# Layer-norm sums by bn_stats, broadcasts by DMA, transposes two products late, and the next slab's gradient of h ahead of each weight gradient, in a fused gated long convolution with its gradients

## The chip, the cores and the metric

The kernel runs on one core of a Trainium2 chip, and the metric is its device time in microseconds (us). One execution computes a forward output and nine gradients. All arrays are bf16 in memory; matrix products accumulate in f32.

## The reference

`x` is 2048 rows by 1024 columns, the three weights connect 1024 and F = 3584 columns. The forward part, cut to what is computed:

```python
xn = (x - mean(x)) / sqrt(var(x) + 1e-5)            # layer norm over the 1024 columns
k_shift = sum over t of k[rows - (3 - t)] * shift_k  # four taps per column
kv  = k_shift * v
y   = irfft(rfft(kv padded to 4096) * rfft(ssm_k padded)) [:2048] + kv * ssm_D
s   = xn * y
h   = (xn @ w_gate) * (xn @ w_up)                    # 2048 x 3584
g   = silu(h @ w_down)
out = x + s * g
```

Then come the gradients of `out`, for a given `grad_out`, by `x`, `k`, `v`, `shift_k`, `ssm_k`, `ssm_D`, `w_gate`, `w_up` and `w_down`. The ten arrays are the outputs.

## The kernel before

Rows are taken in 16 blocks of 128, which make four quarters `q` of 512; the 1024 columns are 8 chunks `dc`; F is 28 chunks `fc` of 128, and two chunks make a slab of 256 columns, of which there are 14. The work follows this order:

- *Start and first two slabs.* `ln_load` fetches the rows of x in chunks of 1, 1, 2, 4, 4 and 4 blocks. `layer_norm` (L408) takes a chunk's row sums on DVE (L412), its sums of squares on ACT (L418), some ten small operations, one of them a square root on ACT (L431), then subtracts and scales each block on DVE (L446, L447), transposes it on PE (L450) and copies the result to `XNT[q]` (L451; the tiles that the trace calls `U`). Once a quarter is there, `gu_unit` multiplies it with the four chunks of the first two slabs. After quarter 0 `build_bcast` (L125) spreads the four taps `shift_k` and the row `ssm_D` to all 128 partitions (`Wbc`, `Dbc`): it copies a tap to a row on one partition (L132), multiplies it with a row of ones on PE (L137), and ACT copies the product from PSUM (L138). After quarter 1 `build_tables` (L145) makes the tables of sines `TF` and, by transposes on PE (L172) and copies on ACT (L173), `TI`.
- *Forward loop.* `gu_unit` (L460) for chunks 4 to 27 and two quarters at a time: four products `psg` of 8 matmuls each (gate and up of each quarter), a copy of each to `gut` on ACT (L472), and on DVE the product `hT` (L478), which goes to memory as `HTd`, and, transposed on PE (L486), as `Hd`. The transposition is a closure `turn` in the list `later`, which `flush` (L456) runs after the next product. After each product `tick` lets `conv_forward`, the convolution by Fourier transforms on PE and DVE, advance by a share of its work: `pump(cnt[0] / NT)` with `NT = 24 * 8.0`, where 192 is the number of products in this loop. What is not done at the end, `drain` does.
- *Middle.* w_down is loaded, `ht` (256 rows of `HTd`) is loaded, and `psbm` = h @ w_down is formed block by block; `gate` makes the output and the gradients that come back through it. `dbm` is transposed into `DBMT` by the same `later` list (L845).
- *Gradient loop*, over the 14 slabs. `dh_half` (L902), four times a slab (two chunks, two halves `hf` of the rows), loads `gul` = the stored gate and up products, forms two products `psdh`, the gradient of h (ACT copies them to `dht`, L913), and on DVE `dgt` = `gul` * `dht` (L917). `dgt` goes to memory, and a `turn` transposes it in two groups of 8 (L925), which ACT copies into `dgu` (L926). `dw_slab` (L929) then forms the gradients of w_up and w_gate: 8 products `psdw` of 16 matmuls, each copied by ACT to `wb` (L937) and stored. `load_wdt` (L891) loads and transposes the slab's rows of w_down. `btick` lets `conv_backward` advance. `dgu` rotates over three tiles.
- *End.* `dwd_slab` forms the gradient of w_down, and the last stage the gradient of xn (`psx`) with the layer norm's backward.

A scheduler puts each engine's instructions into an order of its own choice within what the dependences allow. Loads go by `ld` on SP's queue, most others by `st` and `cld` on POOL's queue; the two first weight slabs are issued by ACT. The loop of the gradients stands as follows:

```python
for sl in range(NSL):
    dgus = []
    for hf in range(2):
        dgu = u8(4 + nd % 3, "p (b a f) -> p b a f", b=8, a=2)
        nd += 1
        for fi in range(2):
            dh_half(2 * sl + fi, hf, wdt, dgu)
        dgus.append(dgu)
    if sl + 1 < NSL:
        wdt = load_wdt(sl + 1)
    flush()
    dw_slab(sl, dgus)
```

Of the kernel before, what the change touches and what calls it, by code (L numbers as in the profile page):

```python
# [19 lines left out]
def build_kernel(  # L20
# [33 lines left out]
    o_dshk, o_dssmk, o_dD, o_dwg, o_dwu, o_dwd = out_4, out_5, out_6, out_7, out_8, out_9  # L54

# [69 lines left out]
    def build_bcast(bps):  # L125
        bsb = pool("bc_sb", 1)
        row = bsb.tile([1, 5, D], BF16, name="row")
        st(row[:, 4, :], A_ssm_D.rearrange("(o d) -> o d", o=1))
        shrow = bsb.tile([1, D, 4], BF16, name="shrow")
        st(shrow[:], A_shift_k.rearrange("(o d) j -> o d j", o=1))  # L130
        for j in range(4):
            nc.vector.tensor_copy(row[0:1, j, :], shrow[0:1, :, j])  # L132
# [7 lines left out]
        nc.vector.memset(zr[:], 0.0)  # L140
# [4 lines left out]
    def build_tables(psp):  # L145
# [20 lines left out]
        for g in range(2):  # L166
            for rp in range(4):
# [5 lines left out]
                nc.scalar.copy(out=TI[:, g, 2 * rp:2 * rp + 2].rearrange("p i k (c u) -> p i k c u", c=2), in_=ps[:])  # L173
        tg.release()


    V = nc.vector
# [230 lines left out]
    def layer_norm(b0, n, x4):  # L408
        def small(name, dt=F32):
            return lns.tile([P, 4], dt, name=name)[:, 0:n]  # L410
        ssum = small("ssum")
        V.tensor_reduce(ssum, x4[:, 0:n, :], AX.X, ADD)  # L412
        negmean = small("negmean")
        V.tensor_scalar(negmean, ssum, -1.0 / D, None, op0=MUL)
        sqs = small("sqs")
        for i in range(n):
            junk = lnp.tile([P, D], BF16, name="junk", bufs=2)
            nc.scalar.activation(junk[:], x4[:, i, :], ACT.Square, bias=negmean[:, i:i + 1], scale=1.0,  # L418
                                 accum_out=sqs[:, i:i + 1])
        mean_b = small("mean_b", BF16)  # L420
        V.tensor_scalar(mean_b, negmean, -1.0, None, op0=MUL)
# [3 lines left out]
        V.tensor_scalar(var_b, sqs, 1.0 / D, None, op0=MUL)  # L425
# [17 lines left out]
        for i in range(n):  # L443
# [7 lines left out]
            V.tensor_copy(XNT[q][:, :, qi * P:(qi + 1) * P], ps[:])  # L451
# [4 lines left out]
    def flush():  # L456
        while later:
            later.pop(0)()
# [135 lines left out]
    for c in xs[:3]:  # L594
        layer_norm(*c)
    for q in range(4):
        if q > 0:
            layer_norm(*xs[q + 2])
# [562 lines left out]
```

## Time and profile before

| | |
|---|---|
| time, median of 3 runs | 2392.72 us (2388.26 to 2396.47) |
| profiled execution: time, span | 2397.11 us, 2395.3 us |
| mean granted TensorE clock of it | 0.979 |
| busy: PE, DVE, ACT, POOL | 92%, 60%, 36%, 25% of the span |
| memory traffic | 450.67 MB, mean 188 GB/s |

PE is TensorE's matmuls (transposes are matmuls too), PEld its weight loads, which run beside them, DVE is VectorE, ACT ScalarE, POOL GpSimd, SP SyncE. A row of a timeline gives start, length, engine, line, operation, out<-in, shapes and count, and in brackets how long the engine stood idle before it and what ended the wait. A row of a waits view gives who waited, for whom, the sum in us, how often, and the longest. A row of a group gives busy us and mean ns behind the bar, then the idle time ahead of the group. A row of stages gives the window, its length, the busy us (and instructions) of PE, PEld, DVE, ACT and POOL, the granted clock, the share of the DMA engines and the GB/s that they moved. The profiler's page cuts the span into 40 slices of 60 us and gives tenths.

### The profile page before, as it was taken

To read this page: it belongs to the slowest core of one execution; us is meant where nothing else is said; L and a number is where in the kernel's file an instruction comes from. 1 tells how busy PE (TensorE), PEld (TensorE's weight loads), DVE (VectorE), ACT (ScalarE), POOL (GpSimd) and SP (SyncE) were. 2 spreads that over 40 slices of the span, in tenths; PEclk is the share of its full clock that TensorE was granted. 3 is DMA by queue.
4 is the path that set the end of the run, shared out by engine and by line. 5 is a ranking of instruction groups with operands and counts; after the bars stand their busy time and mean duration, and the time that the engine had idled before them with its cause. 6 is when DMAs were issued, how large, how long until landed. Compare 5 with 4: busy or idle time off the path is not lost.

```text
span 2395.3 us, 35474 instructions
## 1 busy us (share of the span) xinstructions
PE 2206.5 (92%) x14370; PEld 1185.8 (50%) x14634; DVE 1443.0 (60%) x1941; ACT 863.7 (36%) x1197; POOL 590.7 (25%) x923
## 2 busy tenths in 40 slices
PE   4799999999979997999899989999999999999997
PEld 2456565666634444555455544444454455444443
DVE  8468879796836555666786866777747601322222
ACT  6734443444414234333333334345341152211111
POOL 3532313222202222222344444322224310000000
PEclk9899999999989999999999999999999999999999
DMA  8365747455467657445666566555647665432321
GB/s 271 131 227 177 234 150 257 163 194 180 167 243 258 247 203 280 160 169 138 201 205 217 192 207 223 169 185 195 232 169 239 206 198 187 164 144 101 110 98 35
DMA packets 195285, 450.67 MB, mean 188 GB/s; under 512 B 36224, under 2 KB 93608, under 8 KB 183088
## 3 DMA queue, kind: packets, MB, share of 16 engines
q0 software_dynamic: 71776, 270.11, 32.9%
q1 hardware_dynamic: 119184, 176.18, 22.8%
q8 instruction: 114, 1.87, 0.3%
q10 hardware_dynamic: 4160, 2.10, 0.3%
q14 instruction: 51, 0.42, 0.1%
HBM read 258.48 MB, written 194.02 MB: 189 GB/s over the span
## 4 chain that ended last, share of the span: by engine, by line
PE 41%; issue 25%; DVE 13%; DMA 9%; POOL 6%; ACT 5%; another core or an unknown queue 0%; POOLq 0%; SPq 0%; ACTq 0%; DVEq 0%
PE psx L1049 12%; PE psdw L933 10%; PE psdw L993 5%; PE psg L470 3%; DVE W L185 3%; DMA out_dram<-wb 2%; PE psdh L911 2%; DVE m L185 2%; POOL out_dram L60 2%; PE tr L925 2%; DMA DGUTd<-dgt 1%; PE psbm L808 1%; DVE HX L185 1%; PE tr L981 1%; DMA HFd<-HX 1%
## 5 line engine op out<-in xcount | busy, mean ns | idle before, releaser
L470 PE MATMUL psg<-U,wslab 128*128 128x512 bf16 x1709 | 406.6, 385 | 9.1 <-DVE U L451 3.6
L933 PE MATMUL psdw<-U,U 128*128 128x512 bf16 x1737 | 400.3, 380 | 14.7 <-ACT wb L937 9.3
L1049 PE MATMUL psx<-U,dgut 128*128 128x512 bf16 x1376 | 305.6, 379 | 1.7
L1049 PEld LDWEIGHTS <-dgut 128*128 128x128 bf16 x1792 | 174.7, 98 | 208.1
L933 PEld LDWEIGHTS <-U 128*128 128x128 bf16 x1792 | 172.8, 98 | 199.2 <-issue 9.5
L470 PEld LDWEIGHTS <-wslab 128*128 128x128 bf16 x1792 | 173.0, 99 | 196.5 <-issue 17.8
L60 POOL DMA_DIRECT2D out_dram<-wb x280 | 151.5, 546 | 303.6 <-ACT wb L937 192.0
L472 ACT CAST gut<-psg 128x512 bf16<-128x512 f32 x224 | 131.2, 586 | 250.5 <-PE psg L470 233.0
L185 DVE TENSOR_TENSOR W<-W 128x512 f32<-128x512 f32 (+1 forms) x272 | 213.5, 785 | 7.3
L911 PE MATMUL psdh<-U,wdt 128*128 128x512 bf16 x857 | 210.2, 383 | 5.2 <-ACT dht L913 3.3
L808 PE MATMUL psbm<-U,ht 128*128 128x512 bf16 x875 | 196.9, 382 | 7.7 <-DMA ht<-HTd 6.4
L993 PE MATMUL psdw<-U,U 128*128 128x512 bf16 x873 | 199.3, 380 | 3.5 <-ACT wb L996 1.4
L185 DVE TENSOR_TENSOR W<-W,psP 128x512 f32<-128x512 f32 x192 | 122.6, 683 | 120.7 <-PE psP L234 66.9
L937 ACT CAST wb<-psdw 128x512 bf16<-128x512 f32 x112 | 65.6, 586 | 283.2 <-PE psdw L933 225.1
L185 DVE TENSOR_TENSOR dxn<-psx,dxna_t 128x1024 f32<-128x1024 f32 x16 | 19.6, 1225 | 220.8 <-PE psx L1049 204.3
L926 ACT COPY U<-tr 128x1024 bf16<-128x1024 bf16 x112 | 113.4, 1013 | 84.6 <-PE tr L925 84.4
L808 PEld LDWEIGHTS <-ht 128*128 128x128 bf16 x896 | 87.6, 99 | 110.6 <-DMA ht<-HTd 6.6
L993 PEld LDWEIGHTS <-U 128*128 128x128 bf16 x896 | 86.7, 98 | 100.7 <-issue 2.8
L911 PEld LDWEIGHTS <-wdt 128*128 128x128 bf16 x896 | 84.3, 99 | 84.4 <-issue 5.5
L1065 ACT ACTIVATE junk<-dxn 128x1024 bf16<-128x1024 f32 x16 | 16.9, 1057 | 279.7 <-DVE dxn L185 279.7
L185 DVE TENSOR_TENSOR m<-A,B 128x2048 bf16<-128x2048 bf16 x64 | 75.8, 1221 | 63.6 <-DMA B<-KFd 27.1
L60 POOL DMA_DIRECT2D out_dram<-dx_t x16 | 8.6, 540 | 402.0 <-DVE dx_t L1077 402.0
(250 smaller groups left out, 3105.9 us busy)
## 6 DMA issues: line engine op xcount, KB each, us to landing
gul<-GUTd SPq DMA_DIRECT2D x56, 512.0 KB, 5.4
DGUTd<-dgt POOLq DMA_DIRECT2D x56, 512.0 KB, 6.6
dgut<-DGUTd SPq DMA_DIRECT2D x16, 1792.0 KB, 8.7
GUTd<-gut POOLq DMA_DIRECT2D x48, 512.0 KB, 3.7
A<-DYFd POOLq DMA_DIRECT2D x16, 1024.0 KB, 5.5
ht<-HTd SPq DMA_DIRECT2D x8, 1792.0 KB, 7.4
out_dram<-wb POOLq DMA_DIRECT2D x224, 64.0 KB, 2.1
U<-Hd SPq DMA_DIRECT2D x28, 512.0 KB, 4.2
```

What stands on the lines that cost most here:

```text
L60: return nc.gpsimd.dma_start(out=out, in_=in_)
L185: V.tensor_tensor(o, a, b, op)
L470: nc.tensor.matmul(ps[:], w[:, dc, a, fi * P:(fi + 1) * P], XNT[q][:, dc, :], start=(dc == 0), stop=(dc == DC - 1))
L472: nc.scalar.copy(out=gut[:, a, k * 512:(k + 1) * 512], in_=ps[:])
L808: nc.tensor.matmul(ps[:, dh * 512:(dh + 1) * 512], ht[:, fc, i * P:(i + 1) * P], WD[fc // 4][:, fc % 4, dh * 512:(dh + 1) * 512], start=(f ...
L911: nc.tensor.matmul(ps[:], wdt[:, dc, fi * P:(fi + 1) * P], DBMT[2 * hf + k][:, dc, :], start=(dc == 0), stop=(dc == DC - 1))
L925: nc.tensor.transpose(ps[:, i, :], dgt[:, a, i * P:(i + 1) * P], ident[:])
L926: nc.scalar.copy(out=dgu[:, :, a, fi * P:(fi + 1) * P], in_=ps[:])
L933: nc.tensor.matmul(ps[:].rearrange("p a f -> p (a f)"), XN[b // 4][:, b % 4, dc * P:(dc + 1) * P], dgus[b // 8][:, b % 8].rearrange("p a f ...
L937: nc.scalar.copy(out=wb[:], in_=ps[:])
L993: nc.tensor.matmul(ps[:], h[:, fi, b, :], DBM[b // 4][:, b % 4, dh * 512:(dh + 1) * 512], start=(b == 0), stop=(b == NB - 1))
L1049: nc.tensor.matmul(ps[:, dh * 512:(dh + 1) * 512], t[a][:, 4 * j + f, i * P:(i + 1) * P], WGU[n][:, f, dh * 512:(dh + 1) * 512], start=(n ...
```

## The change

It has seven parts.

1. `layer_norm` gets mean and variance from BN_STATS (two halves of 512 columns a block) and BN_AGGR, both on DVE, in place of the sums on DVE and the squares on ACT. The chunks of x are 2, 2, 4, 4, 4 blocks. The copies to `XNT` may go to any engine (`nc.any`): 10 of the 16 stay on DVE, 6 go to ACT.
2. `build_bcast` has no matmuls and no ACT copies: `Dbc` and a tile `wrow` with the four interleaved taps are loaded by DMAs whose source repeats one row 128 times, on POOL's queue (256 KB and 1 MB), and DVE sorts the taps into `Wbc` by four copies.
3. The copies to `TI` go from ACT to DVE.
4. ACT issues slab 0 alone; slab 1 goes to SP, behind the loads of x and ahead of the copies to `KSLd`.
5. An entry of `later` runs once it has seen two calls of `flush(2)`, that is after the second following product instead of the first. `dw_slab` calls `flush(2)` too, after each of its 8 products.
6. In the loop of the gradients the next slab's `wdt` is loaded first, then come the second half of this slab's gradient of h and the first half of the next slab's, and only then `dw_slab` of this slab.
7. `NT` is smaller by the factor 0.95, so the forward convolution advances faster by 5% and is done 10 products earlier.

Beside these, ACT loads its function table 9 times in place of 6, and one of the 8 copies to `ho` (L755) moves from ACT to DVE.

```diff
-    def build_bcast(bps):
+    def build_bcast():
         bsb = pool("bc_sb", 1)
-        row = bsb.tile([1, 5, D], BF16, name="row")
-        st(row[:, 4, :], A_ssm_D.rearrange("(o d) -> o d", o=1))
-        shrow = bsb.tile([1, D, 4], BF16, name="shrow")
-        st(shrow[:], A_shift_k.rearrange("(o d) j -> o d j", o=1))
+        dsrc, ksrc = A_ssm_D, A_shift_k
+        st(Dbc[:], bass.AP(dsrc.tensor, dsrc.offset, [[0, P], [1, D]]))
+        wrow = bsb.tile([P, D, 4], BF16, name="wrow")
+        st(wrow[:].rearrange("p d j -> p (d j)"), bass.AP(ksrc.tensor, ksrc.offset, [[0, P], [1, 4 * D]]))
         for j in range(4):
-            nc.vector.tensor_copy(row[0:1, j, :], shrow[0:1, :, j])
-        for j in range(5):
-            for dh in range(2):
-                sl = slice(dh * 512, (dh + 1) * 512)
-                ps = bps.tile([P, 512], F32, name="psY")
-                nc.tensor.matmul(ps[:], ones_row[0:1, :], row[0:1, j, sl], start=True, stop=True)
-                nc.scalar.copy(out=(Wbc[:, j, sl] if j < 4 else Dbc[:, sl]), in_=ps[:])
+            V.tensor_copy(Wbc[:, j, :], wrow[:, :, j])
...
-                nc.scalar.copy(out=TI[:, g, 2 * rp:2 * rp + 2].rearrange("p i k (c u) -> p i k c u", c=2), in_=ps[:])
+                V.tensor_copy(TI[:, g, 2 * rp:2 * rp + 2].rearrange("p i k (c u) -> p i k c u", c=2), ps[:])
...
-        ssum = small("ssum")
-        V.tensor_reduce(ssum, x4[:, 0:n, :], AX.X, ADD)
-        negmean = small("negmean")
-        V.tensor_scalar(negmean, ssum, -1.0 / D, None, op0=MUL)
-        sqs = small("sqs")
+        mv = lns.tile([P, 4, 2], F32, name="mv")[:, 0:n, :]
         for i in range(n):
-            junk = lnp.tile([P, D], BF16, name="junk", bufs=2)
-            nc.scalar.activation(junk[:], x4[:, i, :], ACT.Square, bias=negmean[:, i:i + 1], scale=1.0,
-                                 accum_out=sqs[:, i:i + 1])
+            bst = lns.tile([P, 2, 6], F32, name="bst")
+            for hh in range(2):
+                V.bn_stats(out=bst[:, hh, :], in_=x4[:, i, hh * 512:(hh + 1) * 512])
+            V.bn_aggr(out=mv[:, i, :], in_=bst[:])
...
-            V.tensor_copy(XNT[q][:, :, qi * P:(qi + 1) * P], ps[:])
+            nc.any.tensor_copy(XNT[q][:, :, qi * P:(qi + 1) * P], ps[:])
...
-    def flush():
-        while later:
-            later.pop(0)()
+    def defer(fn):
+        later.append([0, fn])
+
+    def flush(age=0):
+
+        for e in later:
+            e[0] += 1
+        while later and later[0][0] >= age:
+            later.pop(0)[1]()
...
-                flush()
+                flush(2)
...
-    slabs = [load_slab(0, nc.scalar), load_slab(1, nc.scalar)]
-    chunks = [(0, 1), (1, 1), (2, 2), (4, 4), (8, 4), (12, 4)]
+    slabs = [load_slab(0, nc.scalar)]
+    chunks = [(0, 2), (2, 2), (4, 4), (8, 4), (12, 4)]
     xs = [(b0, n, ln_load(b0, n)) for (b0, n) in chunks]
+    slabs.append(load_slab(1, nc.sync))
...
-    NT = 24 * 8.0
+    NT = 0.95 * 24 * 8.0
...
             st(o_dwu[dc * P:(dc + 1) * P, fs], wb[:, 1, :])
+            flush(2)
             btick(2)
...
+    def dh_slab_half(sl, hf, wdt):
+        dgu = u8(4 + (2 * sl + hf) % 3, "p (b a f) -> p b a f", b=8, a=2)
+        for fi in range(2):
+            dh_half(2 * sl + fi, hf, wdt, dgu)
+        return dgu
+
+    first = dh_slab_half(0, 0, wdt)
     for sl in range(NSL):
-        dgus = []
-        for hf in range(2):
-            dgu = u8(4 + nd % 3, "p (b a f) -> p b a f", b=8, a=2)
-            nd += 1
-            for fi in range(2):
-                dh_half(2 * sl + fi, hf, wdt, dgu)
-            dgus.append(dgu)
+        wnext = load_wdt(sl + 1) if sl + 1 < NSL else None
+        dgus = [first, dh_slab_half(sl, 1, wdt)]
         if sl + 1 < NSL:
-            wdt = load_wdt(sl + 1)
-        flush()
+            first = dh_slab_half(sl + 1, 0, wnext)
+        else:
+            flush()
+        wdt = wnext
         dw_slab(sl, dgus)
```

How this moves instructions shows at three places. Numbers behind a tile's name tell its buffers apart; `x` with a number is one chunk of its rows. The first place is DVE's queue at the start, as the third and fourth block of x are finished. Before, the scaling of a block (L447), then single operations of `build_bcast` (L132), of the next chunk's sums (L412) and the copies to `XNT` follow each other:

```order
L447 TENSOR_SCALAR x_147<-x_147,RSTD 128x1024
L441 CAST sq_f<-sq_b 128x1
L427 TENSOR_SCALAR vpe_b<-var_b 128x2
L446 TENSOR_SCALAR x_151<-x_151,mean_f 128x1024
L442 RECIPROCAL RSTD<-sq_f 128x1
L429 CAST vpe<-vpe_b 128x2
L132 COPY row<-shrow 1x1024
L451 COPY U_113<-tr 128x8x128
L447 TENSOR_SCALAR x_149<-x_149,RSTD 128x1024
L433 RECIPROCAL rr_274<-r__272 128x2
L414 TENSOR_SCALAR negmean<-ssum 128x4
L412 TENSOR_REDUCE ssum<-x_155 128x4
```

Now, on DVE at the same place (L179 is the helper for two-tensor operations, L134 the sorting of the taps, L438 the scaling):

```order
L410 BN_AGGR mv<-bst 128x2
L409 BN_STATS bst<-x_148 128x6
L179 TENSOR_TENSOR r_247<-r__241,q_245 128x2
L134 COPY Wbc<-wrow 128x1024
L430 TENSOR_SCALAR sq_b<-r_247 128x2
L134 COPY Wbc<-wrow 128x1024
L432 CAST sq_f<-sq_b 128x2
L134 COPY Wbc<-wrow 128x1024
L433 RECIPROCAL RSTD<-sq_f 128x2
L134 COPY Wbc<-wrow 128x1024
L438 TENSOR_SCALAR x_146<-x_146,RSTD 128x1024 x2
L409 BN_STATS bst<-x_148 128x6 x2
```

The four copies of `Wbc` stand between the second chunk's square root and the scaling that follows from it, so that scaling comes behind the load of `wrow`.

The second place is SP's queue at the end of the forward loop, where the last slab, the w_down rows and the first `ht` are loaded. Before:

```order
L399 DMA wslab<-in_B_w_gate_dram 128x8x256
L57 DMA U_113<-in_B_w_down_dram 128x4x1024
L57 DMA U_114<-in_B_w_down_dram 128x4x1024
L57 DMA U_115<-in_B_w_down_dram 128x4x1024
L57 DMA U_116<-in_B_w_down_dram 128x4x1024
L57 DMA U_7845<-in_B_w_down_dram 128x4x1024
L57 DMA U_7846<-in_B_w_down_dram 128x4x1024
L57 DMA U_7847<-in_B_w_down_dram 128x4x1024
L57 DMA ht<-HTd 128x7168
```

Now, on SP:

```order
L393 DMA wslab<-in_B_w_gate_dram 128x8x256
L59 DMA U_113<-in_B_w_down_dram 128x4x1024
L59 DMA U_114<-in_B_w_down_dram 128x4x1024
L59 DMA U_115<-in_B_w_down_dram 128x4x1024
L59 DMA ht<-HTd 128x7168
L59 DMA U_116<-in_B_w_down_dram 128x4x1024
L59 DMA U_7795<-in_B_w_down_dram 128x4x1024
L59 DMA U_7796<-in_B_w_down_dram 128x4x1024
L59 DMA U_7797<-in_B_w_down_dram 128x4x1024
```

`ht` has moved ahead of four of the seven loads.

The third place is ACT's queue in the middle of the gradient loop, from the last products of the gradient of h into the weight gradient. Before (`yl` belongs to the convolution's backward):

```order
L913 CAST dht<-psdh 128x512 x3
L926 COPY U_7847<-tr 128x8x128 x2
L913 CAST dht<-psdh 128x512
L926 COPY U_7845<-tr 128x8x128
L913 CAST dht<-psdh 128x512
L926 COPY U_7845<-tr 128x8x128
L899 COPY wdt<-tr 128x8x128 x2
L729 CAST yl<-psY 128x512
L926 COPY U_7845<-tr 128x8x128 x2
L729 CAST yl<-psY 128x512
L937 CAST wb<-psdw 128x512 x7
```

Now, on ACT:

```order
L897 COPY wdt<-tr 128x8x128 x2
L911 CAST dht<-psdh 128x512 x4
L924 COPY U_7797<-tr 128x8x128 x2
L911 CAST dht<-psdh 128x512 x2
L924 COPY U_7797<-tr 128x8x128 x2
L911 CAST dht<-psdh 128x512 x2
L924 COPY U_7795<-tr 128x8x128 x2
L935 CAST wb<-psdw 128x512
L727 CAST yl<-psY 128x512 x2
L935 CAST wb<-psdw 128x512
L924 COPY U_7795<-tr 128x8x128 x2
L935 CAST wb<-psdw 128x512 x3
```

Each transposed `dgt` (L924) comes after one more pair of `dht` copies, and the last of the group stands between the weight gradient's first `wb` copies; `wdt` is ahead of the group, where it stood behind.

More of the change, by code (lines that the diff above doesn't have):

```diff
@@ L54, in build_kernel @@
     o_dshk, o_dssmk, o_dD, o_dwg, o_dwu, o_dwd = out_4, out_5, out_6, out_7, out_8, out_9
+    V = nc.vector
     def ld(out, in_):
@@ L489, in turn @@
             st(Hd[fc, :, 4 * qs[0]:4 * qs[0] + nb, :], h[:, 0:nb, :])
-        later.append(turn)
+        defer(turn)
     def conv_forward():
@@ L593, in build_kernel @@
            kin[:, ds * P:(ds + 1) * P].rearrange("(p a) d -> p a d", a=16))
-    for c in xs[:3]:
+    for c in xs[:2]:
         layer_norm(*c)
@@ L597, in build_kernel @@
         if q > 0:
-            layer_norm(*xs[q + 2])
+            layer_norm(*xs[q + 1])
         for fc in range(4):
@@ L601, in build_kernel @@
         if q == 0:
-            build_bcast(ps_y)
+            build_bcast()
         if q == 1:
@@ L846, in turn @@
             nc.scalar.copy(out=DBMT[b // 4][:, :, (b % 4) * P:(b % 4 + 1) * P], in_=ps[:])
-        later.append(turn)
+        defer(turn)
     def load_ht(bp):
@@ L926, in turn @@
                 nc.scalar.copy(out=dgu[:, :, a, fi * P:(fi + 1) * P], in_=ps[:])
-        later.append(turn)
+        defer(turn)
     def dw_slab(sl, dgus):
@@ L940, in dw_slab @@
             st(o_dwu[dc * P:(dc + 1) * P, fs], wb[:, 1, :])
+            flush(2)
             btick(2)
```

9 lines of the change are left out of this document (3 added, 6 removed).

## The prediction

> **What bounds the kernel now.** I read the page first (engines, slices), then stages cut where PE's line changes, then who PE waits for, then the places themselves.
>
> ```profile
> PE 2206.5 (92%) x14370; PEld 1185.8 (50%) x14634; DVE 1443.0 (60%) x1941; ACT 863.7 (36%) x1197; POOL 590.7 (25%) x923
> PEclk9899999999989999999999999999999999999999
> ```
>
> PE is the bound, and time falls only where PE now stands still or runs at half rate. By stage (length; busy PE, PEld, DVE, ACT, POOL; granted clock, DMA share, GB/s):
>
> ```profile
> 0.00:34.00 34.00, 9.43 (x42) 4.11 (x43) 27.14 (x75) 18.31 (x35) 5.06 (x17) 1.00 0.99 297
> 34.00:133.00 99.00, 76.82 (x468) 40.94 (x476) 62.50 (x102) 69.66 (x98) 56.77 (x71) 0.90 0.53 175
> 133.00:671.00 538.00, 508.65 (x4465) 319.82 (x4540) 436.79 (x564) 225.93 (x350) 138.10 (x207) 0.99 0.57 193
> 671.00:694.00 23.00, 8.37 (x74) 7.12 (x73) 9.83 (x13) 3.95 (x6) 3.11 (x4) 0.59 1.00 369
> 910.00:1722.00 812.00, 752.47 (x5030) 409.51 (x5123) 576.77 (x726) 332.06 (x453) 273.68 (x436) 0.98 0.60 196
> ```
>
> They are: the start; the stage in which four blocks of rows at a time are normalized and multiplied by the first two slabs (34 to 133); the forward loop; its end; and the loop over slabs of the gradient of h and the weight gradients. The change touches no other stage. The longest waits of PE and of its weight loads over the whole run, and then those of the forward loop alone (us in total, times, longest):
>
> ```profile
> PE tr L925 <- DVE dgt L185: 31.5, 18, 5.5
> PE tr L486 <- DVE hT L185: 29.9, 31, 3.4
> PEld L925 <- DVE dgt L185: 46.2, 32, 6.0
> ...
> PE tr L486 <- DVE hT L185: 20.0, 26, 2.5
> PEld L486 <- DVE hT L185: 31.4, 32, 3.0
> ```
>
> The two largest are transposes (of dgt, of hT) that wait for the vector engine's last product; the true stall lies between PE's number and PEld's, since both count the same pause. One of them, in order of time:
>
> ```profile
> 196.86 0.59 ACT L472 CAST gut<-psg 128x512 bf16<-128x512 f32 x1 [1.14 <-PE psg L470]
> 198.59 0.59 ACT L472 CAST gut<-psg 128x512 bf16<-128x512 f32 x1 [1.14 <-PE psg L470]
> 200.01 0.69 DVE L185 TENSOR_TENSOR hT<-gut 128x1024 bf16<-128x1024 bf16 x1
> 200.75 0.98 PE L486 MATMUL tr<-ident,hT 128*128 128x128 bf16 x8 [2.21 <-DVE hT L185]
> 200.00:205.00 5.00, 4.25 (x18) 2.10 (x19) 4.97 (x8) 1.20 (x2) 1.32 (x2) 0.66 0.38 129
> ```
>
> A product is 1.73 us (198.59 − 196.86). PE stood 2.2 us, and the clock over the next 5 us was 0.66: some 3.4 us at half rate, 1.7 us more lost.
>
> **The change part by part.** *Start.* Ones-row matmuls leave PE, squares leave ACT, BN_STATS comes to DVE, the rows come spread by DMA.
>
> ```profile
> 4.06 1.22 DVE L412 TENSOR_REDUCE ssum<-x 128x1 f32<-128x1024 bf16 x1 [2.48 <-DMA x<-in_A_q_dram]
> 9.19 2.29 DVE L412 TENSOR_REDUCE ssum<-x 128x2 f32<-128x2048 bf16 x1 [0.99 <-DMA x<-in_A_q_dram]
> 14.11 1.15 ACT L418 ACTIVATE junk<-x,negmean 128x1024 bf16<-128x1024 bf16 x1 [11.38 <-issue]
> 17.23 0.67 DVE L132 COPY row<-shrow 1x1024 bf16<-1x1024 bf16 x1
> 20.37 0.47 DVE L447 TENSOR_SCALAR x<-x,RSTD 128x1024 bf16<-128x1024 bf16 x1
> 34.04 6.79 PE L470 MATMUL psg<-U,wslab 128*128 128x512 bf16 x23 [0.25 <-DVE U L451]
> ```
>
> Before, ACT could not start until 14.11 (it was issuing slabs). Four blocks of x (1 MB) were there at 9.19, beside 1 MB of slab: 2.1 MB at 297 GB/s is 7.1 us, so 2.1 us are fixed. Now 1 MB of slab 0 and 1.3 MB of broadcast (128 copies of 2 KB and of 8 KB) share the time, if the three queues share alike: 3.4 MB, 11.5 + 2.1, about 13.6. Then DVE's order up to the fourth block's scaling: 9 BN_STATS, 8 TENSOR_SCALAR at 0.47 (3.8), 4 copies of Wbc at 0.67 (2.7), some 24 small ones at about 0.1 (2.4). No row shows BN_STATS; half of a 1.22 us reduction of 1024 is 0.61, the nearest (5.5 for nine); a whole reduction, 1.22, is the upper end. Together 14.4, and with transposes and a copy the first product comes near 28.5: **−5.5** (0 with 1.22 us each; −10 if the broadcast doesn't delay x). That Wbc's copies stand ahead of the fourth block's RSTD in DVE's queue makes the late landing of wrow the danger here; KSLd's loads move behind slab 1, and POOL's k loads with them, which nothing needs before 100 us.
>
> *34 to 133.* The worst hole of the trace:
>
> ```profile
> 78.45 1.95 PE L172 MATMUL tr<-ident,TF 128*128 128x128 bf16 x32
> 94.66 3.66 PE L450 MATMUL tr<-ident,x 128*128 128x128 bf16 x32 [0.94 <-ACT TI L173]
> 99.09 2.10 PE L470 MATMUL psg<-U,wslab 128*128 128x512 bf16 x8 [0.78 <-DVE U L451]
> L418 ACT ACTIVATE junk<-x,negmean 128x1024 bf16<-128x1024 bf16 x16 | 18.4, 1157 | 11.4 <-issue 11.4
> L173 ACT COPY TI<-tr 128x1024 bf16<-128x1024 bf16 x8 | 7.8, 1022 | 0.0
> L451 DVE COPY U<-tr 128x1024 bf16<-128x1024 bf16 x16 | 10.5, 685 | 11.3 <-PE tr L450 11.3
> L431 ACT ACT_TABLE_LOAD x2 | 2.6, 1283 | 0.0
> ```
>
> ACT, interleaving sines and TI copies, held PE for 20 us. It loses 18.4 of squares and 7.8 of TI, and gains 6 copies of XNT at 1.0 and 3 table loads at 1.3. DVE takes TI at 0.69, 5.5 us more; 16 reductions of 1.22 and 32 BN_STATS of 0.61 are equal. What hides it is DVE's idle time, 36 of 99 us; were it gone, the 5.5 us would come on top. The stage has 22 us in which PE is idle, and a clock that lacks 0.10 on the mean, 10 us, of which I put half on PE's busy time: 27 in all. The normalization of the next four blocks still ends in a chain on DVE that PE waits for, so I take half: **−13** (0 to −24). The Trainium skill, "VectorE: DVE Perf Modes", Specifications, says that VectorE sits closer to SBUF and ScalarE to PSUM, which speaks against moving PSUM copies of TI to DVE. The rows above disagree: 685 ns on DVE, 1022 on ACT for the same shape. By the rule the eight copies would cost DVE 8.2 us instead of 5.5.
>
> *Forward loop.* The transposes come one product later: 1.73 us more slack. Of this loop's waits (20.0 by PE, 31.4 by PEld) the longest is 3.0, so nearly all could go: I take 24. But DVE is full in places:
>
> ```profile
> 360.00:420.00 60.00, 56.96 (x420) 32.05 (x427) 58.75 (x71) 23.75 (x37) 21.54 (x32) 1.00 0.78 261
> ```
>
> There (98%) more slack helps nothing, and three such stretches hold about half the waits: −12. Three half-rate spells like that at 200 go with them: 3 × 1.7 = −5. NT × 0.95 puts the convolution's DVE work into 5% fewer products: in the 180 us of full DVE some 3 products (1.9 each with transposes) are pushed out to the end, +6. **−11** (−25 if all waits go; +18 if the loop is DVE's everywhere, since 10 products then run alone). By the Trainium skill, "TensorE: Matmul & The Clock Gate", Part 1, the half rate follows an idle window of about 3.4 us; the trace shows it after 2.2. By the rule the 5 us would not be these waits' and would stay, as in (e) below.
>
> *End of the forward loop.*
>
> ```profile
> 665.83 5.34 PE L470 MATMUL psg<-U,wslab 128*128 128x512 bf16 x23
> 678.05 1.01 PE L331 MATMUL psY<-KX,TI 128*128 128x128 bf16 x8 [4.33 <-DVE KX L188]
> 679.97 0.34 SPq L57 DMA_DIRECT2D ht<-HTd  x1
> 693.85 0.61 PE L808 MATMUL psbm<-U,ht 128*128 128x512 bf16 x1 [6.38 <-DMA ht<-HTd]
> HTd<-hT POOLq DMA_DIRECT2D x48, 256.0 KB, 4.3
> ht<-HTd SPq DMA_DIRECT2D x8, 1792.0 KB, 7.4
> ```
>
> From the last product's end (671.2) to the first psbm is 22.7 us: the inverse transform's last steps, then ht issued behind seven w_down loads and 13.9 us under way. Now the transform is over before, and ht stands ahead of four of the loads: hT 1.4, its store 0.8 + 4.3, ht 7.4, about 14. The 3.4 us of psY matmuls move ahead, so 22.7 − 14 − 3.4: **−5** (0 if ht takes 13.9 again, −10 if it overlaps). The half clock behind the gap stays.
>
> *Gradient loop.* Every transposition of dgt gets one more product, and the last of a slab, on which the weight gradient waits, four more. Its longest waits:
>
> ```profile
> 923.46 0.45 PEld L925 LDWEIGHTS <-dgt 128*128 128x128 bf16 x8 [4.85 <-DVE dgt L185]
> 1386.69 0.77 PEld L925 LDWEIGHTS <-dgt 128*128 128x128 bf16 x8 [6.01 <-DVE dgt L185]
> 1560.10 0.77 PEld L925 LDWEIGHTS <-dgt 128*128 128x128 bf16 x8 [5.54 <-DVE dgt L185]
> ```
>
> After 1.73 these three leave 11.2; the other 29 (29.8 us, at most 2.6 each) leave about 2. So 33 us go by PEld's count of 46.2, and 18 by PE's of 31.5; between them I take **−24** (−8 if DVE's lateness returns at the next transposition, −35 with the clock). DVE is busy 71% here, which hides the same 56 products of dgt. wdt's transposes, the loads (gul, wrow) on SP and the stores on POOL are the same in number, one half-slab apart; their cover is the 28 us of each weight gradient. Deferred work that falls late in a weight gradient is covered by its next 16 matmuls.
>
> Sum: −5.5 −13 −11 −5 −24 = −58.5. The profiled execution took 2397.1 (span 2395.3), the median of three runs 2392.7, 4 lower; on the median's scale 2334.
>
> **The rivals.** (a) *DVE takes PE's place* in the forward loop: for it speaks the full stretch at 360 and 437 of 538 us busy, against it that DVE is idle 101 us. Then the loop gives +18 − 8 (the drained tail) instead of −16: 2334 + 26 = 2360. (b) *All stalls go with their half clocks*: the lower ends, −10 −24 −25 −10 −35 = −104, 2289; near it the stage from 34 must be PE's alone. (c) *Nothing*: PE is freed at one transposition and stands at the next as long: 2393 ± 7. For it speaks that DVE's queue, not the product, ended the wait at 200. (d) *Slower*: each of 14 weight gradients now begins with a deferred dgt; if DVE is so late that PE stands there as at 923 (4.85 us and 1.7 of half clock), 14 × 6.55 = 92 come in place of −24: 2334 + 24 + 92 = 2450. It decides from 3.0 us a slab (34.5 of other gains and 7 over, by 14). Against it: the deferred product has two products of 3.5 us each, and DVE is idle 235 of 812 us. (e) *The half-rate spells stay*, since something other than these waits brings them: 2334 + 5 = 2339; against it that the spell at 200 begins within the wait. The page on the clock gate named above is for it, with its longer window.
>
> **How the numbers follow.** Forecast 0.48 and (e) 0.08 (together 2310 to 2358), (a) 0.17, (b) 0.13, (c) 0.06, (d) 0.08. The 8-in-10 range leaves out (c), (d) and the far part of (b): 2295 to 2376. About 0.3%, 7 us, is what a measurement here can tell. Faster is forecast, (a), (b) and (e), 0.86; same is (c), 0.06; slower (d), 0.08.
>
> **What would show it.** First psg near 28; no TI wait of PE and second-column products without a hole at 78 to 99; DVE's BN_STATS near 0.6 us; waits of tr for hT under 12 us and for dgt under 15; first psbm some 14 us after the last psg; granted clock 0.98 to 0.99 overall. Wrong if BN_STATS takes over 1.2 us, if wrow lands after 20 us, if PE's waits for DVE turn up under other names (psS, psY, psg) in the same sum, or if PE waits for DVE at the head of each weight gradient.

## The result, and the profile after

The changed kernel takes 2338.27 us, median of 4 runs (2333.64 to 2340.01), against 2394.15 (2388.26 to 2396.47) before: a ratio of 0.9767, 95% interval 0.9744 to 0.979. The forecast was 2334. Its profiled execution took 2340.01 us with a span of 2338.2, 57.1 less than the span before. From its page, the engines:

```profile
PE 2202.9 (94%) x14624; PEld 1182.1 (51%) x14624; DVE 1445.6 (62%) x1969; ACT 833.9 (36%) x1154; POOL 591.8 (25%) x922
```

PE's busy time is the same within 4 us: what went is time in which PE stood. ACT lost 30 us, and DVE gained only 3: BN_STATS and BN_AGGR took 24 us there in place of the 18 of the reductions, and the copies of TI 5, while the copies to `XNT` that went to ACT took 4 off. To see where the time went, both runs are cut at the same events: the first product `psg`, the last matmul of the first two slabs' products, the last matmul `psg` of the forward loop, the first `psdh`, and the first product of w_down's gradient. (Chunk 4's first product follows right behind the second cut before, and 3.0 us behind it after, since PE waits there 1.56 us for hT and 0.60 for a copy; these 3.0 us are counted in the loop.) The rows of before and after for the stages that moved (columns as in the prediction):

```profile
34.04:131.80 97.76, 76.49 (x468) 40.89 (x476) 62.46 (x102) 69.13 (x96) 56.73 (x70) 0.90 0.52 172
131.80:670.60 538.80, 508.58 (x4466) 319.70 (x4540) 436.38 (x564) 226.42 (x350) 138.10 (x207) 0.99 0.57 194
911.90:1726.80 814.90, 754.22 (x5042) 410.53 (x5134) 580.49 (x727) 332.83 (x455) 273.67 (x436) 0.98 0.60 197
```

```profile
0.00:24.60 24.60, 3.77 (x32) 3.25 (x32) 17.23 (x60) 4.83 (x7) 8.61 (x20) 1.00 0.97 332
24.60:121.60 97.00, 77.45 (x470) 41.84 (x471) 74.40 (x143) 61.78 (x81) 52.59 (x65) 0.88 0.66 203
121.60:662.70 541.10, 515.64 (x4610) 324.86 (x4609) 443.92 (x576) 226.08 (x354) 140.31 (x209) 0.99 0.57 193
889.40:1671.00 781.60, 751.45 (x5137) 408.42 (x5134) 582.67 (x728) 326.68 (x454) 274.37 (x437) 0.99 0.62 206
```

| stage | before | after | moved | forecast |
|---|---|---|---|---|
| start, to the first psg | 34.0 | 24.6 | −9.4 | −5.5 |
| first two slabs | 97.8 | 97.0 | −0.8 | −13 |
| forward loop, to its last psg matmul | 538.8 | 541.1 | +2.3 | −11 |
| its end and the middle, to the first psdh | 241.3 | 226.7 | −14.6 | −5 |
| gradient loop | 814.9 | 781.6 | −33.3 | −24 |
| the rest | 668.5 | 667.2 | −1.3 | 0 |
| span | 2395.3 | 2338.2 | −57.1 | −58.5 |

So the sum came out, but not its parts: the second and third rows fell short by 12 and 13 us, and the start, the loop's end and the gradient loop made up for it. The errors of the five terms add up to some 50 us; that their sum misses by 1.4 is luck. Four executions whose first two stages are the same program (this one and experiments 2, 3 and 4) end the second at 118.0 to 121.6 us; a difference of 3 us in one profiled stage is not read as an effect below.

The forward loop's waits of PE before (us in total, times, longest), the same after, and the gradient loop's after, by PE and by its weight loads:

```profile
PE tr L486 <- DVE hT L185: 20.0, 26, 2.5
...
PE psY L331 <- DVE KX L188: 0.7, 3, 0.4
```

```profile
PE tr L483 <- DVE hT L179: 10.9, 9, 2.0
PE psY L325 <- DVE KX L182: 10.0, 8, 2.8
```

```profile
PE tr L923 <- DVE dgt L179: 9.2, 9, 3.6
PE tr L896 <- ACT wdt L897: 5.8, 2, 5.1
PE psdw L931 <- ACT wb L935: 4.9, 1, 4.9
PE tr L923 <- ACT U L924: 1.5, 2, 1.3
...
PEld L923 <- DVE dgt L179: 14.6, 12, 4.1
```

The wait for hT lost 9 us and the wait of the inverse transform for its input KX gained 9. The wait for dgt went from 31.5 to 9.2 by PE and from 46.2 to 14.6 by its weight loads, and nothing of that size took its place; the largest new wait is the 5.8 for `wdt`.

In the stage of the first two slabs the hole at 78 to 99 is gone with its TI waits, and a new one stands at 76 to 88. First PE's rows there, then the chain that it waits for, in order of time:

```profile
75.63 0.61 PE L168 MATMUL tr<-ident,TF 128*128 128x128 bf16 x8
83.73 3.60 PE L441 MATMUL tr<-ident,x 128*128 128x128 bf16 x32 [7.48 <-DVE x L438]
```

```profile
65.60 0.20 ACT L422 ACTIVATE r__820<-vpe 128x4 f32<-128x4 f32 x1
68.02 2.91 DVE L179 TENSOR_TENSOR prod<-k,Wbc 128x2048 bf16<-128x2048 bf16 x1
71.18 0.16 DVE L424 RECIPROCAL rr<-r__820 128x4 f32<-128x4 f32 x1
72.38 0.15 DVE L179 TENSOR_TENSOR q<-vpe,rr 128x4 f32<-128x4 f32 x1
78.16 1.56 DVE L179 TENSOR_TENSOR r<-r__820,q 128x4 f32<-128x4 f32 x1
80.78 0.15 DVE L430 TENSOR_SCALAR sq_b<-r 128x4 bf16<-128x4 f32 x1
82.77 0.16 DVE L432 CAST sq_f<-sq_b 128x4 f32<-128x4 bf16 x1
83.18 1.68 DVE L438 TENSOR_SCALAR x<-x,RSTD 128x1024 bf16<-128x1024 bf16 x4
```

The third quarter's square root was done on ACT at 65.8. Six links follow on DVE (the last, RSTD, ahead of the scaling), five of about 0.15 us and one, at 78.16, of 1.56, and took until 83: 17.4 us from the square root's end to the scaling. DVE took up its queue in order, and between the links stand the convolution's shift products (`prod`, `acc`), copies of TI (six of the eight, 3.8 us) and the tables' `mm`.

### The profile page after: what moved, and what is told of

Same layout as the page of the kernel before. It is cut to its first block, busy times and chain, and to the rows that moved or that the text cites. A ratio compares the mean times of both kernels' runs of the same rounds, so it can differ in the third digit from the quotient of the medians.

```text
span 2338.2 us, 35695 instructions
## 1 busy us (share of the span) xinstructions
PE 2202.9 (94%) x14624; PEld 1182.1 (51%) x14624; DVE 1445.6 (62%) x1969; ACT 833.9 (36%) x1154; POOL 591.8 (25%) x922
## 4 chain that ended last, share of the span: by engine, by line
PE 42%; issue 7%; DMA 5%; ACT 3%; DVE 2%; POOL 2%; POOLq 0%; ACTq 0%; SPq 0%; DVEq 0%
PE psx L1051 14%; PE psdw L931 11%; PE psdw L995 6%; PE psdh L909 4%; DMA out_dram<-wb 2%; PE tr L923 2%; POOL out_dram L62 1%; PE tr L983 1%; ACT U L924 1%; DVE W L179 1%; PE psY L747 1%; PE psY L785 1%; DMA DGUTd<-dgt 1%; DMA B<-HFd 1%; ACT wb L935 1%
## 5 line engine op out<-in xcount | busy, mean ns | idle before, releaser
L467 PE MATMUL psg<-U,wslab 128*128 128x512 bf16 x1792 | 418.1, 386 | 8.7 <-ACT gut L469 3.8
L931 PE MATMUL psdw<-U,U 128*128 128x512 bf16 x1792 | 407.8, 381 | 4.9 <-ACT wb L935 4.9
L179 DVE TENSOR_TENSOR W<-W 128x512 f32<-128x512 f32 (+1 forms) x272 | 213.4, 785 | 7.3
L995 PE MATMUL psdw<-U,U 128*128 128x512 bf16 x896 | 202.4, 381 | 3.0 <-DMA U<-Hd 1.7
L179 DVE TENSOR_TENSOR W<-W,psP 128x512 f32<-128x512 f32 x192 | 122.8, 683 | 102.5 <-ACT W L259 54.0
L179 DVE TENSOR_TENSOR dxn<-psx,dxna_t 128x1024 f32<-128x1024 f32 x16 | 19.6, 1225 | 220.8 <-PE psx L1051 220.7
L924 ACT COPY U<-tr 128x1024 bf16<-128x1024 bf16 x112 | 113.6, 1014 | 45.6 <-PE tr L923 45.6
L179 DVE TENSOR_TENSOR m<-A,B 128x2048 bf16<-128x2048 bf16 x64 | 75.7, 1222 | 65.7 <-DMA B<-KFd 32.2
```

Source lines behind the costliest of these rows:

```text
L179: V.tensor_tensor(o, a, b, op)
L467: nc.tensor.matmul(ps[:], w[:, dc, a, fi * P:(fi + 1) * P], XNT[q][:, dc, :], start=(dc == 0), stop=(dc == DC - 1))
L924: nc.scalar.copy(out=dgu[:, :, a, fi * P:(fi + 1) * P], in_=ps[:])
L931: nc.tensor.matmul(ps[:].rearrange("p a f -> p (a f)"), XN[b // 4][:, b % 4, dc * P:(dc + 1) * P], dgus[b // 8][:, b % 8].rearrange("p a f ...
L995: nc.tensor.matmul(ps[:], h[:, fi, b, :], DBM[b // 4][:, b % 4, dh * 512:(dh + 1) * 512], start=(b == 0), stop=(b == NB - 1))
```

## The experiments

Each kernel was timed beside runs of the kernel before; to compare them with each other, the ratio to before is given with its 95% interval, and the stages of the profiles. Each has one profile.

**1. hT transposed one product late again.** In `gu_unit`, all else as changed:

```diff
-                flush(2)
+                flush()
```

> The changed kernel (2338 us), with only this undone: in the forward loop the transposition of hT runs after the next product again, not after the second. Theory A (the second product is real slack): PE's waits for hT return from 15 to 25 to 30 us and the loop, 541 us from the first product of chunk 4 to the start of the last one, becomes 549 to 555; the gap at its end stays at 9 us; the whole 2346 to 2352. Rival (DVE sets the loop, so a wait for hT that goes comes back at the convolution's psY): hT's waits return, psY's waits fall from 10 us by as much, the loop stays within 3 us of 541 and the whole within 4 us of 2338.

2349.32 us, ratio 0.9807 (0.9779 to 0.9835). The loop took 546.9 us:

```profile
PE tr L483 <- DVE hT L179: 21.0, 19, 3.3
PE psY L325 <- DVE KX L182: 5.7, 7, 1.4
```

Between the two theories: hT's wait rose by 10.1, psY's fell by 4.3, and the difference, 5.8, is what the loop got longer (546.9 − 541.1). So by these two profiles DVE gives back some 40% of the wait that is taken away in this loop. The whole lies where theory A had it, 11 us above the changed kernel, though the loop lost only 5.8; the other stages lost about 1 us each.

**2. The convolution at its old pace.**

```diff
-    NT = 0.95 * 24 * 8.0
+    NT = 24 * 8.0
```

> The changed kernel with the forward convolution at its old pace (NT without the factor 0.95). Theory A (the pace, and nothing else, put the first ht load ahead of four w_down loads, and PE's new waits for psY within the loop are its price): the gap between the last psg product and the first psbm goes from 9 back to 20 to 23 us, PE's psY waits fall from 10 to 5 us, the loop gets 6 to 10 us shorter (531 to 535), the whole 2341 to 2347. Rival (the later hT transposition moved ht): gap 9 to 12 us, the whole 2330 to 2338.

2338.03 us, ratio 0.9765 (0.9738 to 0.9792), as the changed kernel. The order of SP's queue is the old one, `ht` behind all seven w_down loads, and the profile has the loop and the gap behind it as follows:

```profile
118.70:641.70 523.00, 501.47 (x4474) 319.12 (x4544) 435.35 (x565) 223.55 (x350) 138.86 (x208) 1.00 0.59 200
641.70:666.80 25.10, 7.75 (x75) 6.43 (x73) 10.60 (x13) 3.94 (x6) 3.10 (x4) 0.65 0.99 361
```

The gap went back, to 25.1 us (9.6 in the changed kernel by the same cut), and the loop got 18 us shorter; theory A gave the gap 20 to 23 and the loop 6 to 10. Some 5 of the loop's 18 us are the clock, which is 1.00 here without a half-rate spell and 0.99 with three in the changed kernel; PE's waits for KX are 5.3 us (10.0 there). From the end of the first two slabs to the first psbm it is 548 us here and 551 in the changed kernel: the pace moves the convolution's tail from the gap into the loop, and pays for nothing. Theory A had the place of ht right, and was wrong that it brings time.

**3. The gradient loop in its old order**, with two products of slack kept:

```diff
-    first = dh_slab_half(0, 0, wdt)
     for sl in range(NSL):
-        wnext = load_wdt(sl + 1) if sl + 1 < NSL else None
-        dgus = [first, dh_slab_half(sl, 1, wdt)]
+        dgus = [dh_slab_half(sl, hf, wdt) for hf in range(2)]
         if sl + 1 < NSL:
-            first = dh_slab_half(sl + 1, 0, wnext)
-        else:
-            flush()
-        wdt = wnext
+            wdt = load_wdt(sl + 1)
+        flush()
```

> The changed kernel with the gradient loop in its old order (both halves of a slab's gradient of h, then its weight gradient, with all deferred transpositions run ahead of it); two products of slack within the halves stay. Theory A (the last dgt of a slab, on which the weight gradient waits, was less than half of the loss): the gradient loop, 781.6 us now and 814.9 before, becomes 790 to 800, PE's waits for dgt go from 9 to 16 to 22 us, the whole 2346 to 2356. Rival (the order carries the gain): the loop goes back to 805 to 815, the whole 2362 to 2372. Second rival (the order is worth nothing beside the slack): 780 to 785, the whole 2335 to 2342.

2366.1 us, ratio 0.9882 (0.9856 to 0.9907); the loop 806.0 us; both are the first rival's. Its waits of PE:

```profile
PE psdw L931 <- ACT wb L935: 16.5, 7, 8.6
PE tr L923 <- DVE dgt L179: 13.7, 9, 3.5
PE tr L923 <- ACT U L924: 5.1, 13, 1.9
```

The wait for dgt is only 4.5 us longer. What returned is ACT, 15 us more: the deferred transpositions, and those of `wdt`, come close together, 1.7 us apart, among the first products of the weight gradient, where 13 of them wait for the one PSUM tile that ACT copies out in 1.0 us (2 did), and the weight gradient's products wait seven times for a copy to `wb` (one did; the longest, 8.6, falls where the store of experiment 12 is under way). Against that, the 5.8 us of waits for `wdt` are gone. The other 10 us of the 24.4 are spread, and why the copies are late more often was not followed further.

**4. The new order, but dgt transposed one product late.** `flush(2)` becomes `flush()` in `dh_half` and `dw_slab`.

> The changed kernel with its new order of the gradient loop, but dgt transposed after the next product, as before, not after the second. Theory A (both parts are needed): the loop 781.6 becomes 795 to 805, PE's waits for dgt 20 to 30 us, the whole 2352 to 2362. Rival (the order carries the gain): 780 to 787, the whole 2337 to 2344. Second rival (the slack carries it): 808 to 815, the whole 2364 to 2372.

2358.3 us, ratio 0.9847 (0.9819 to 0.9874); the loop 802.5, both as theory A had them, and the wait for dgt is back:

```profile
PE tr L923 <- DVE dgt L179: 25.3, 17, 4.2
```

From before, slack alone is worth 814.9 − 806.0 = 8.9 us, order alone 12.4, both 33.3: each takes away a wait that the other leaves.

**5. The layer norm's sums as before**, all else as changed: the lines of `layer_norm` that the diff removes stand in place of BN_STATS and BN_AGGR.

> The changed kernel with the layer norm's sums as before (row sums on DVE, squares on ACT), all else as changed. First psg now 24.6, before 34.0; the stage of the first two slabs 97 us now, 98 before. Theory B (the start's gain came from the broadcast, whose ones-row products PE and ACT no longer have ahead of them; BN_STATS only frees ACT in the stage that follows): first psg 25 to 28, the stage 103 to 110 us, the whole 2344 to 2354. Rival (BN_STATS made the start's gain): first psg 30 to 33, the whole 2344 to 2360. Second rival (ACT's squares never held anything): first psg 25 to 28 and the stage 95 to 99, the whole 2336 to 2341.

2342.32 us, ratio 0.9805 (0.9786 to 0.9824). The first psg comes at 36.9, later than in any of the other kernels; the stage ends at 124.8.

```profile
14.29 4.42 DVE L406 TENSOR_REDUCE ssum<-x 128x4 f32<-128x4096 bf16 x1 [2.36 <-DMA x<-in_A_q_dram]
18.62 0.16 DVE L419 TENSOR_SCALAR var_b<-sqs 128x2 bf16<-128x2 f32 x1
86.60 3.60 PE L444 MATMUL tr<-ident,x 128*128 128x128 bf16 x32 [7.15 <-DVE x L441]
```

Theory B fell: BN_STATS made the start's gain, and more than the rival gave it (36.9 for 30 to 33; the whole is 2 us below its range). The old sum of the third chunk, one instruction of 4.4 us that waits 2.4 us for its data, stands ahead of the first chunk's variance. But the 12.3 us by which the first psg moves are worth 3.2 us at the stage's end, since the transposes of the third quarter's x begin at 86.6 here and at 83.7 in the changed kernel: the start was not what set the end.

**6. The broadcast as before**, by ones-row products and ACT copies (the old `build_bcast`), BN_STATS kept.

> The changed kernel with the taps and ssm_D spread as before (a row of ones on PE, copies of the products on ACT), BN_STATS kept. Theory B: first psg goes from 24.6 back to 30 to 34 us, the stage behind it stays at 94 to 99, the whole 2343 to 2349. Rival (BN_STATS made the start's gain): first psg 24 to 27, the whole 2337 to 2342.

2340.86 us, ratio 0.9794 (0.9774 to 0.9814). First psg at 24.3, the rival's number; the stage 102 us, 5 longer, with PE's waits for ACT's table `TF` (9.0 us) in place of those for x. By time the two versions can't be told apart.

**7. The broadcast after quarter 2**, so that DVE's shift products come later:

```diff
-        if q == 0:
+        if q == 2:
             build_bcast()
```

> The changed kernel with the broadcast written after quarter 2 instead of quarter 0, so that the four Wbc copies and the convolution's first shift products (k by Wbc) come later in DVE's queue. Theory C (the hole of 7.5 us that PE has near 76 to 84 us, and the half clock behind it, come from DVE's queue: shift products of 1.2 us, and longer ones beside POOL's integer products, stand between the small links of the third quarter's normalization): first psg 21.5 to 23 (2.7 us of copies leave its chain), the stage 97 becomes 85 to 91, the whole 2322 to 2331. Rival (the hole is the chain's own length, or ACT's sines and table loads): first psg 21.5 to 23, the stage 95 to 99, the whole 2334 to 2339. Against both: shift products pushed into the forward loop, up to 8 us on it.

2327.25 us, ratio 0.9739 (0.9722 to 0.9755). Theory C held: the stage took 82 us, with the clock at 0.96 in place of 0.88, and no shift product stands between the links. From the square root's end (49.15) to the scaling it is 3.9 us in place of 17.4, and the square root itself comes 16.7 us earlier. Only the first psg, at 23.7, came later than the 21.5 to 23 expected. The forward loop, 542.1 against 541.1, lost nothing that one profile can tell.

```profile
23.72:105.80 82.08, 73.94 (x475) 38.90 (x475) 61.35 (x133) 60.22 (x80) 48.16 (x62) 0.96 0.74 227
48.95 0.20 ACT L422 ACTIVATE r__805<-vpe 128x4 f32<-128x4 f32 x1
53.01 1.67 DVE L438 TENSOR_SCALAR x<-x,RSTD 128x1024 bf16<-128x1024 bf16 x4
```

**8. Each quarter's normalization written ahead of the products before it.** `layer_norm` runs for three chunks ahead of the loop, and in it for chunk q + 2.

> The changed kernel with each quarter's normalization written ahead of the products of the quarter before it (quarter 1's ahead of all products), the broadcast where it is. Theory C: the third quarter's chain is through before DVE gets to the shift products, the hole near 76 us closes, the stage 97 becomes 85 to 91; first psg 24 to 26; the whole 2326 to 2333. Rival (the hole is the chain's own length or ACT's): the stage 94 to 99, the whole 2335 to 2341.

2333.63 us, ratio 0.9765 (0.9742 to 0.9787): the stage 92 us, between the two theories. PE's hole of 7.5 us is gone, and the third quarter's x is transposed from 54.8 on (83.7 in the changed kernel). But here the shift products stay in the stage: DVE is busy for 80 of its 92 us (61 of 82 in 7), and PE's waits are spread over `gut` (4.9 us), TI (3.1) and x (2.8). So closing the hole gave 5 of the 15 us of experiment 7, and the other 10 came only where the shift products left the stage too.

**9. TI copied by ACT again.**

```diff
-                V.tensor_copy(TI[...], ps[:])
+                nc.scalar.copy(out=TI[...], in_=ps[:])
```

> The changed kernel with the copies to TI on ACT again, as before; broadcast and normalization as changed. Theory (ACT's sines, table loads and TI copies of 1.0 us each held PE in the kernel before; on DVE they take 0.7): PE's waits for TI come back, 4 to 10 us; DVE loses 5.5 us of work in the hole's stretch, so the stage of the first two slabs, 97 us now, becomes 95 to 104; the whole 2336 to 2346. Rival (TI belongs on ACT, since it is DVE's queue that holds the third quarter): the stage 85 to 92, the whole 2326 to 2333.

2346.56 us, ratio 0.9798 (0.9774 to 0.9822). PE waits for TI again, 9.4 us, and the stage takes 100 us. The hole that follows is now ACT's: DVE stands 9.4 us for the third quarter's square root, which on ACT comes behind four copies of TI (83.27 to 87.01) and a table load:

```profile
82.37 1.01 PE L168 MATMUL tr<-ident,TF 128*128 128x128 bf16 x8 [6.54 <-ACT TI L169]
88.56 0.18 DVE L424 RECIPROCAL rr<-r__820 128x4 f32<-128x4 f32 x1 [9.36 <-ACT r__820 L422]
90.33 4.00 PE L441 MATMUL tr<-ident,x 128*128 128x128 bf16 x46 [6.95 <-DVE x L438]
```

The rival, that TI belongs on ACT, fell. But the stage's 3 us are no effect by themselves, and explain only part of the 8 in the median; where the rest is, stays open. The intervals of this ratio and of the changed kernel's overlap, so that DVE is the better place is not shown by time.

**10. Three products of slack** for hT and dgt, on top of 7 (`flush(3)`).

> The changed kernel with the broadcast after quarter 2 (2327 us as measured) and with transpositions of hT and dgt after the third following product, not the second. Theory D (what is left of the waits for hT and dgt, 18.6 and 12.7 us by PE, is lateness of one more product's length): they fall to 6 to 10 and 4 to 7 us, the forward loop 542 becomes 530 to 536, the gradient loop 785 becomes 776 to 781, the whole 2308 to 2319. Rival (what is left stands where DVE is full over many products, so more slack only moves it to psY, psP and psS): both loops within 3 us, the whole 2323 to 2331.

2332.4 us, ratio 0.9751 (0.9731 to 0.9771). The forward loop took 547.7 us, some 5 longer, the gradient loop 783.1, 2.1 shorter. In the latter the wait for dgt is nearly gone, and another has come:

```profile
PE tr L923 <- ACT U L924: 22.4, 8, 9.6
...
PE tr L923 <- DVE dgt L179: 3.6, 4, 2.0
```

Theory D fell. The rival held in kind, though its 3 us and its 2331 were missed by 2 and by 1: a third product brings nothing, and with it PE waits for the one PSUM tile of the transpositions instead (the 9.6 at the place where experiment 12 moves a store).

**11 and 12. The best version again, and one store of it moved** to SP's queue:

```diff
-        st(o_dD.rearrange("(c p) -> p c", p=P), ddo[:])
+        ld(o_dD.rearrange("(c p) -> p c", p=P), ddo[:])
```

> The changed kernel with the broadcast after quarter 2, once more and in more rounds, as the best version so far: 2324 to 2330 us by the first look (2327.25).

> The same kernel, with one store moved from POOL's queue to SP's: the 2 KB of the gradient of ssm_D (1024 pieces of 2 bytes), which takes 21.6 us to land. In the gradient loop ACT waits 11.6 us for two stores of wb that were issued behind it, and PE 6.4 us for ACT, with some 6.8 us at half clock behind. Theory E (the stores wait in the queue behind it): PE's wait goes, the gradient loop 785 becomes 775 to 779, the whole 2317 to 2322. Rival (the small pieces fill the DMA engines themselves, whichever queue they come by): the wait of PE stays at 5 to 8 us, the whole 2324 to 2330.

2331.53 us (2324 to 2330 were expected), ratio 0.973 (0.9717 to 0.9744), and 2329.14, ratio 0.9723 (0.9709 to 0.9736). In the second PE waits as long as without the move (5.3 us there):

```profile
PE psdw L931 <- ACT wb L935: 4.9, 1, 4.9
```

The gradient loop took 787.1 us, against 785.2 without the move, and the store landed 22.1 us after its issue from SP's queue, 21.6 from POOL's. So theory E fell, and the rival stands: the queue is not what holds the others. That the store itself does is read from the times alone, since no run left it out.

The version of experiment 7 stands at 0.9739 and, measured again, at 0.973; the changed kernel stands at 0.9767. The intervals overlap or touch at their edges, so the gain, 7 to 11 us in the whole, is not sure by time alone; at the end of the first two slabs both profiles have it, 14 to 16 us.

## Why the prediction was right, point by point

The total, 2338.27 for 2334, is right in part by luck. Two of the five terms failed, those of the first two slabs and of the forward loop; three gave more than forecast; the errors cancelled. What held is the view that PE's own work stays and that the time lies in its waits, those for dgt above all.

- *Start, −9.4 for −5.5.* BN_STATS took 0.66 us where half of a reduction gave 0.61. The term that was mis-sized is the landing of the first four blocks of x, put at 13.6 since the broadcast was to share the time: they were there at 9.15, as before (9.19), so the broadcast did not delay them, which is the prediction's own lower end. From there to the end of the fourth block's scaling it was 13.1 us for "14.4 together", and transposes and copies took 2.4 where the forecast had left 0.5:

```profile
9.15 0.69 DVE L409 BATCH_NORM_STATS2 bst<-x 128x6 f32<-128x512 bf16 x1 [1.05 <-DMA x<-in_A_q_dram]
21.34 0.87 DVE L438 TENSOR_SCALAR x<-x,RSTD 128x1024 bf16<-128x1024 bf16 x2
```

  The rows of `wrow` did not come late: its first copy began at 18.46 without a wait. By experiment 5 the term meant little for the end.
- *Stage of the first two slabs, −0.8 for −13: this step failed.* Two of its parts were right: ACT no longer holds PE, and the copies of TI took 5.1 us on DVE, 0.68 each, as the rows had it. The failed step is "what hides it is DVE's idle time": an average over 99 us said that DVE had 36 us to spare, but the third quarter's chain has to pass through DVE's queue link by link, behind shift products and the very copies of TI that had come over, and the gap simply went to the next holder (experiment 7: 15 us come out of the stage when the shift products leave). The prediction had named the chain and taken half for it; it took all.
- *Forward loop and its end, together −12.3 for −16; the loop alone +2.3 for −11, which failed.* Half of hT's wait went, as forecast, but it bought no time in the loop: the 9.1 us came back as 9.3 for KX, the prediction's own sign of being wrong ("under other names"). About 4 of them are the slack's by experiment 1, about 5 the pace's by experiment 2. The term for the end was wrong in mechanism: `ht` did not follow the last hT and its store. It was issued at 660.11, 3 us ahead of the last product's end, because it needs only rows that were done long before, and now stands ahead of the load into `U_116`, which must wait for that product:

```profile
660.11 0.34 SPq L59 DMA_DIRECT2D ht<-HTd  x1
663.28 10.38 SPq L59 DMA_DIRECT2D U<-in_B_w_down_dram  x4
672.33 33.54 PE L806 MATMUL psbm<-U,ht 128*128 128x512 bf16 x146 [7.05 <-DMA ht<-HTd]
```

  The gap fell from 22.7 to 9.1 us where 14 was forecast, by more than the forecast's own limit of 10, and the loop paid for it: the "+6" for NT × 0.95 was too small (18 by experiment 2, of which some 5 are the clock), and the two are worth nothing together. What is left of the −12.3 is the slack's, −6.8 by experiment 1 over the same stretch (774.6 us there, 767.8 here), and the rest lies near what one profile can tell.
- *Gradient loop, −33.3 for −24.* Here the mechanism was right, and the size lay in the choice between PE's count of the waits and that of its weight loads. Their fall is 22.3 and 31.6 us; the loads' count is the nearer one. But the forecast laid it all on dgt, and by experiment 3 24.4 of the 33.3 go when the order goes. There only 4.5 us of waits for dgt came back, and 15 for ACT's copies, which no term named (5.8 for `wdt` went).
- *The half-rate spells, rival (e).* The forecast took three of them, 5 us, away with the waits. There are still three in the forward loop, near 130, 205 and 502, behind waits of 2.3, 2.8 and 2.0 us, two of which are new ones, for a slab and for KX. The three waits of PE, and the clock behind the last:

```profile
128.94 2.61 PE L467 MATMUL psg<-U,wslab 128*128 128x512 bf16 x8 [2.29 <-DMA wslab<-in_B_w_gate_dram]
204.30 0.61 PE L325 MATMUL psY<-KX,TI 128*128 128x128 bf16 x8 [2.76 <-DVE KX L182]
501.16 0.62 PE L483 MATMUL tr<-ident,hT 128*128 128x128 bf16 x8 [1.97 <-DVE hT L179]
502.00:505.40 3.40, 3.40 (x9) 1.22 (x8) 2.25 (x4) 1.42 (x2) 2.15 (x4) 0.51 0.98 394
```

  So it need not be a wait for hT, and rival (e) was right in that part of its reason. The number of spells says little: in experiment 7's kernel one profile has two and the other one, and experiment 2's has none. That (e)'s 2339 fits the time is luck too. The Trainium skill, "TensorE: Matmul & The Clock Gate", Part 1, has the half rate come after an idle window of about 3.4 us; this row has it after 1.97.
- *The rivals.* (a), DVE as the bound of the forward loop, is partly true: 40% of a wait taken away comes back, and a third product of slack brings nothing. (b) and (c) did not come: 57 us went, neither 104 nor none. (d) did not come either: the longest wait for dgt in the loop is 3.6 us, nine in all, and the weight gradients' products waited once, 4.9 us, for a copy to `wb`.

## What to carry to other kernels

When one engine holds another by a serial chain, ask of the next engine not how idle it is on the mean but what stands in its queue between the chain's links: here 17 us passed over six short links, and moving later work out of the way (one line) took 15 us out of the stage, where a start 12 us earlier had been worth 3. Deferring work by a second step paid here and by a third did not, since the wait moved to the one tile that the deferred work shares; and two remedies for one wait (slack, and order) have to be tried together, since each alone gave about a third of what they gave together (27 and 37%).

## What the runs showed of the hardware

Small operations on DVE took ten times their time beside an integer product on POOL. In the stage of the hole, a copy of 128x4, else 0.12 to 0.15 us, took 1.88 and ended with POOL's product (64.6 for both); the chain's product at 78.16 took 1.56 and ended at 79.72, POOL's next one at 79.69.

```profile
62.72 1.88 DVE L414 CAST mean_f<-mean_b 128x4 f32<-128x4 bf16 x1
61.27 3.31 POOL L152 TENSOR_TENSOR m<-f,tcol 128x1024 int32<-128x1024 int32 x1 [0.88 <-DVE mean_b L412]
```

The Trainium skill, "SBUF — State Buffer", section on its two separate sides, has DVE and GpSimd share a pair of ports that one of them locks for a whole instruction; the row agrees, though no run here took POOL's work away.

While a store of 2 KB in 1024 pieces of 2 bytes is under way, the DMA engines are busy at little traffic, from POOL's queue and from SP's alike (experiment 12: busy throughout the 14 us from 1096, at 62 GB/s); no run left the store out. In experiment 7's kernel, while PE waited:

```profile
out_dram<-ddo POOLq DMA_DIRECT2D x1, 2.0 KB, 21.6
1092.00:1106.00 14.00, 10.45 (x83) 5.96 (x82) 10.28 (x16) 3.59 (x5) 1.61 (x3) 1.00 0.84 52
```

The engines are busy for 84% of these 14 us and move 52 GB/s, where the gradient loop as a whole has 62% and 206.
